# Idle products in four float32 passes of up to 384 columns, in place of one float32r pass of up to 512

## The chip, the cores and the metric

The kernel runs on one core of a Trainium2 chip. The core has five engines that work side by side and meet by semaphores: TensorE (PE in the profile; its weight loads are shown apart as PEld) multiplies matrices, VectorE (DVE), ScalarE (ACT) and GpSimd (POOL) work element by element, and SyncE (SP) issues most of the transfers. The metric is the time of one execution on the device in microseconds (us), less being better. Runs of the kernel before took 491.94 to 493.27 us, with a median of 492.61.

## What is computed

An attention layer of the RWKV-6 kind, then a channel mixer with a residual. The shapes are 4 batches, 8 heads, 768 time steps and a head of 48; the mixer works on 768 x 384 values a batch and widens them to 1536.

```
for t in range(S):                                  # state: (B, H, D, D), starts at 0
    cur = einsum('bhd,bhe->bhde', u * k[t], v[t])
    y[t] = einsum('bhd,bhde->bhe', r[t], state + cur)
    state = w[t][..., None] * state + einsum('bhd,bhe->bhde', k[t], v[t])
x  = y as (B, S, H * D)
xn = (x - mean(x)) / sqrt(var(x) + 1e-6) * g_ln
out = x + maximum(xn @ w_ch1, 0) @ w_ch2
```

## The kernel before

The work is cut into eight rounds: a batch and one half of its 768 steps, so 384 steps (three tiles of 128) for all eight heads. In each round the attention is computed in blocks of 64 steps. Within a block, pairs of sub-blocks are joined level by level (the tile `a` in PSUM takes the small products `a<-r,k`), the keys times the values give the state after each block (`a<-v,k`, then a scan `s` on VectorE), and `a<-v,A`, `a<-vx,A` and `a<-s,r` give the outputs. Then come the normalization (`xn`, its transpose `xT_ps`, and `xf`), the first product of the mixer into `h_ps`, the relu into `h`, and the second product into `o` with the residual. The first round loads and converts the weights of the mixer beside this (`raw`, `held`, `w1`, `ffn2`). In rounds 0 to 3 the second product is done with plain float32 operands (`o<-ffn,h`, 12 chunks for each of the three tiles of a round). In later stages products are split into parts of type float32r (`h_ps<-xhl,wh` and the like).

Every operation is entered into a plan with a cost, and the list `ORDER` (from line 76) fixes the order in which the operations are issued, on which engine each of them goes, and so what every engine's stream of instructions looks like. `Plan.order` (from line 241) goes through the list once, computes when each operation would start by the costs, and gives each tile its place. It also keeps a count of the instructions that TensorE has had (`count`), takes from it where the stream of instructions crosses an edge between pieces of `PIECE` = 256 instructions, and adds a wait where the piece would not have come (`fetches`). These computed times are used for three things that change the program: the places of tiles, the order of semaphore waits, and the idle products.

Idle products are products of zeros by zeros into a PSUM bank that nobody reads. Where the plan sees TensorE without work for more than 0.35 us, it puts n units of them (each 0.24 us by the plan; half as many for the time up to 5.9 us) ahead of the next operation of TensorE, and adds `4 * -(-n // 3)` to its count of instructions. The function `idle` near the end of the kernel makes the products. Before the change, it takes one width for all products of a run: 512 columns where n is divisible by 3, 384 where the remainder is 1, 256 where it is 2, and as many products of that width as fit. Their operand is `nought_r`, one zero a partition of type float32r, read with a stride of nothing as 128 x 128 weights and as the moving columns. `nought_r` is made by ScalarE from `nought`, which VectorE sets to zero as its first instruction. ScalarE's next instructions are a square root that brings its table in (`root`), the clearing of a PSUM tile, and a load of the first tile of k (`nat_k`) on its own queue.

All engine calls go through one helper, so nearly all instructions have line 47 in the profile, and groups are told apart by the names of their tiles.

## Time and profile before

| | us |
|---|---|
| median of 3 runs | 492.61 |
| lowest and highest | 491.94, 493.27 |
| the profiled execution | 492.7 |
| its span, first to last instruction | 490.9 |
| share of the TensorE clock granted | 0.999 |

The profile is of one execution. Its span leaves out 1.8 us around the first and the last instruction. A group's row gives the engine, the operation, the tiles as output<-inputs, the shape and the count, then the busy time in us and the mean length of one in ns, then the idle time of the engine just before, with what ended it. In the timeline the first number is the start and the second the length of the merged stretch, and square brackets hold the idle time before it and what ended it. "issue" means that an engine stood still and the profile shows nothing that it waited for. A window's row has, for each engine, the busy time and the number of instructions that ran in it, then the granted clock, the busy share of the DMA engines and GB/s. Products of TensorE overlap, and their ends are modelled. Queue 8 in the list of the DMA queues has the kind "instruction": it brings code. Semaphore waits that are instructions of their own stand in an engine's stream, but not in the counts of the views.

### The profile page before, as it was taken

To read this page: it belongs to the slowest core of one execution; us is meant where nothing else is said; L and a number is where in the kernel's file an instruction comes from. 1 tells how busy PE (TensorE), PEld (TensorE's weight loads), DVE (VectorE), ACT (ScalarE), POOL (GpSimd) and SP (SyncE) were. 2 spreads that over 40 slices of the span, in tenths; PEclk is the share of its full clock that TensorE was granted. 3 is DMA by queue.
4 is the path that set the end of the run, shared out by engine and by line. 5 is a ranking of instruction groups with operands and counts; after the bars stand their busy time and mean duration, and the time that the engine had idled before them with its cause. 6 is when DMAs were issued, how large, how long until landed. Compare 5 with 4: busy or idle time off the path is not lost.

```text
span 490.9 us, 17279 instructions
## 1 busy us (share of the span) xinstructions
PE 475.5 (97%) x7409; PEld 410.1 (84%) x7409; DVE 352.4 (72%) x727; ACT 257.5 (52%) x593; POOL 126.0 (26%) x136
## 2 busy tenths in 40 slices
PE   7898999999999999998999999999999999999995
PEld 6677988666987779976789877789999999999995
DVE  6999999999956838776776976856967552532544
ACT  5988888536452444372238515158753543533440
POOL 3113107033215163322115120001241241130210
PEclk9999999999999999999999999999999999999999
DMA  7887774675494831382572251053212210232201
GB/s 220 208 229 174 223 173 127 174 203 138 107 246 84 217 58 52 107 207 45 132 206 83 42 81 51 16 158 100 82 34 64 81 49 21 78 97 80 81 1 49
DMA packets 105469, 56.23 MB, mean 115 GB/s; under 512 B 61872, under 2 KB 102320, under 8 KB 105392
## 3 DMA queue, kind: packets, MB, share of 16 engines
q1 hardware_dynamic: 105120, 54.92, 43.0%
q8 instruction: 58, 0.95, 0.8%
q10 hardware_dynamic: 272, 0.20, 0.2%
q14 instruction: 19, 0.16, 0.1%
HBM read 45.27 MB, written 7.47 MB: 107 GB/s over the span
## 4 chain that ended last, share of the span: by engine, by line
PE 81%; DVE 11%; issue 2%; ACT 2%; DMA 1%; SPq 1%; POOL 1%; DVEq 0%; POOLq 0%
PE h_ps L47 27%; PE a L47 23%; PE o L47 19%; PE o_2P L47 3%; PE k_ps L47 2%; DVE A L47 2%; PE o_2D L47 2%; PE r_ps L47 2%; PE xT_ps L47 2%; DVE vals L47 2%; DMA raw<-in_moe_w_ch_dram 1%; DVE s L47 1%; PE kn_ps L47 1%; SPq L47 1%; DVE nat_k L47 1%
## 5 line engine op out<-in xcount | busy, mean ns | idle before, releaser
L47 PE MATMUL o<-ffn,h 128*128 128x384 f32 x288 | 100.4, 490 | 0.0
L47 ACT ACTIVATE h<-h_ps 128x384 f32<-128x384 f32 (+2 forms) x108 | 47.9, 456 | 67.5 <-PE h_ps L47 67.0
L47 PEld LDWEIGHTS o<-ffn,h 128*128 128x128 f32 x288 | 52.0, 190 | 28.3
L47 ACT ACTIVATE h_ps<-h_ps 128x384 f32<-128x384 f32 x84 | 39.2, 478 | 52.3 <-PE h_ps L47 51.0
L47 PE MATMUL h_ps<-xd,d 128*128 128x384 f32 x204 | 50.5, 354 | 0.7 <-DVE x L47 0.7
L47 POOL TENSOR_TENSOR hL<-h,hH 128x384 fp32r<-128x384 f32 x24 | 25.7, 1078 | 89.2 <-ACT hH L47 32.9
L47 DVE SCALAR_TENSOR_TENSOR hD<-hH,hL 128x384 fp32r<-128x384 f32 x48 | 31.0, 664 | 24.1 <-PE a L47 10.3
L47 PEld LDWEIGHTS a<-r,k 48*56 48x56 f32 (+3 forms) x3072 | 39.5, 122 | 9.7 <-issue 3.2
L47 PE MATMUL a<-r,k 48*56 48x32 f32 (+3 forms) x3072 | 43.6, 208 | 0.9 <-ACT k L47 0.9
L47 PE MATMUL h_ps<-xhl,wl 128*128 128x384 f32 x180 | 43.9, 352 | 0.0
L47 PE MATMUL h_ps<-xhl,wh 128*128 128x384 f32 x180 | 41.5, 338 | 0.1
L47 DVE TENSOR_TENSOR k<-k,tot 112x768 f32<-112x768 f32 (+1 forms) x40 | 31.5, 790 | 12.3 <-PE a L47 12.1
L47 DVE TENSOR_TENSOR r<-r,tot 112x768 f32<-112x768 f32 (+1 forms) x40 | 34.4, 863 | 6.6 <-PE a L47 5.1
L47 PEld LDWEIGHTS h_ps<-xd,d 128*128 128x128 f32 x204 | 35.5, 188 | 3.1 <-DVE x L47 1.0
L47 DVE TENSOR_TENSOR hL<-h,hH 128x384 fp32r<-128x384 f32 x24 | 13.8, 584 | 27.6 <-ACT hH L47 14.6
L47 PEld LDWEIGHTS h_ps<-xhl,wh 128*128 128x128 f32 x180 | 32.2, 188 | 0.5 <-issue 0.5
L47 PEld LDWEIGHTS h_ps<-xhl,wl 128*128 128x128 f32 x180 | 31.1, 188 | 1.4
L47 ACT COPY A<-a 32x384 f32<-32x384 f32 (+5 forms) x60 | 25.3, 426 | 7.2 <-PE a L47 5.4
L47 ACT ACTIVATE xf<-xT_ps,g_sb 128x384 f32<-128x384 f32 (+2 forms) x27 | 14.5, 547 | 27.1 <-PE xT_ps L47 20.4
L47 ACT ACTIVATE hH<-h 128x384 fp32r<-128x384 f32 x48 | 23.4, 518 | 6.9 <-issue 4.9
L47 PE MATMUL h_ps<-xf,w 128*128 128x128 f32 (+1 forms) x144 | 25.7, 332 | 0.0
L47 POOL TENSOR_TENSOR nat_r<-pad_k,pad_r 128x576 f32<-128x576 f32 (+1 forms) x9 | 15.0, 1668 | 40.5 <-DVE nat_k L47 38.3
(184 smaller groups left out, 1090.3 us busy)
## 6 DMA issues: line engine op xcount, KB each, us to landing
d<-w1d SPq DMA_DIRECT2D x84, 192.0 KB, 2.5
raw<-in_moe_w_ch_dram SPq DMA_DIRECT2D x24, 384.0 KB, 3.7
nat_w<-in_w_dram SPq DMA_DIRECT2D x24, 192.0 KB, 3.7
nat_r<-in_r_dram SPq DMA_DIRECT2D x24, 192.0 KB, 3.4
v<-in_v_dram SPq DMA_DIRECT2D x24, 192.0 KB, 3.9
nat_k<-in_k_dram SPq DMA_DIRECT2D x23, 192.0 KB, 3.4
w1d<-w1diff SPq DMA_DIRECT2D x12, 192.0 KB, 3.6
out_dram<-x SPq DMA_DIRECT2D x4, 576.0 KB, 4.8
```

The source lines that it names most:

```text
L47: ins = self.tc.keep_in_program_order(f(*args, **kw))
```

## The change

The zeros stay float32, the copy to float32r is dropped, and a run of n idle units is made of products of up to three units, 128 columns a unit.

```diff
     nought = const.tile([P, 1], F32, name="nought")
     DVE.memset(nought, 0.0)
-    nought_r = const.tile([P, 1], F32R, name="nought_r")
-    ACT.copy(out=nought_r, in_=nought)
+    zeros = nought.broadcast_to([P, P])
...
     def idle(n, home):
         t = banks.tile([P, 512], F32, tag=f"b{home}", name="idle")
-        cols = 512 - 128 * (n % 3)
-        for _ in range(max(n * 576 // (cols + 38), 1)):
+        while n:
+            now = min(n, TT)
             PE.matmul(
-                t[:, 0:cols], nought_r.broadcast_to([P, P]), nought_r.broadcast_to([P, cols]),
-                start=True, stop=True,
+                t[:, 0 : now * P], zeros, nought.broadcast_to([P, now * P]), start=True, stop=True
             )
+            n -= now
```

`TT` is 3 and `P` is 128. Nothing in the plan changes: neither `ORDER`, nor the costs, nor the number of units n of each run, nor the places of the tiles. Every other operation stays as it was and in its order.

## The prediction

> **What bounds the kernel now.** The page first, then the chain of waits, then the waits and the timeline at three places.

> ```profile
> span 490.9 us, 17279 instructions
> PE 475.5 (97%) x7409; PEld 410.1 (84%) x7409; DVE 352.4 (72%) x727; ACT 257.5 (52%) x593; POOL 126.0 (26%) x136
> q8 instruction: 58, 0.95, 0.8%
> PE 81%; DVE 11%; issue 2%; ACT 2%; DMA 1%; SPq 1%; POOL 1%; DVEq 0%; POOLq 0%
> ```

> TensorE (PE) carries 81% of the chain that ended last, VectorE (DVE) 11%. The idle products fill the first 40 us only, where the chain runs over VectorE and the loads:

> ```profile
> DVE rk L47 <- DMA nat_k<-in_k_dram: 2.6, 1, 2.6
> DVE pad_k L47 <- DMA nat_k<-in_k_dram: 0.6, 1, 0.6
> ```

> These are the two longest of VectorE's waits for data in the first 50 us; the third is for a load too, and none is for TensorE. So the idle products themselves lie on no path. The chain has 2% of "issue", about 10 us (0.02 x 490.9), and three pieces of it in the later part stand out:

> ```profile
> 194.42 0.13 issue
> ...
> 223.07 1.48 issue
> ...
> 327.81 0.72 issue
> ```

> The second, seen in the timeline:

> ```profile
> 222.42 0.64 PE L47 MATMUL a<-v,k 64*48 64x48 f32 x40
> 224.54 0.30 PE L47 MATMUL a<-v,k 64*48 64x48 f32 x8 [1.48 <-issue]
> 224.98 0.32 DVE L47 COPY s<-a 112x48 f32<-112x48 f32 x2 [3.83 <-PE a L47]
> ```

> One group of 48 products, all of whose inputs were there for the first 40, stops in its middle. That is no wait for data. The windows between the three points at which TensorE goes on tell what it is:

> ```profile
> core 0: us, PE busy (x) PEld busy (x) DVE busy (x) ACT busy (x) POOL busy (x), PEclk, DMA share, GB/s
> 194.50:224.50 30.00, 28.52 (x636) 24.37 (x636) 20.08 (x35) 16.80 (x37) 10.84 (x11) 1.00 0.58 147
> 224.50:328.50 104.00, 103.13 (x2165) 80.97 (x2165) 80.01 (x167) 42.40 (x94) 20.66 (x23) 1.00 0.35 85
> ```

> Products and weight loads are 2 x 636 = 1272 from the first point to the second and 2 x 2165 = 4330 from the second to the third. Queue 8 moved 0.95 MB in 58 packets, 16.4 KB each; TensorE's 2 x 7409 = 14,818 instructions over 58 are about 256 a packet. 5 x 256 is 1280 and 17 x 256 is 4352: both counts fall short by 8 and 22, and TensorE's stream also holds waits on semaphores, which the views do not count. So all three stops lie on one grid of 256 instructions: TensorE ran out of code at a piece's edge and waited for queue 8. From the edge before to the point where it goes on:

> ```profile
> 191.28:194.55 3.27, 3.14 (x148) 2.78 (x137) 1.68 (x6) 0.85 (x2) 1.07 (x2) 1.00 0.02 5
> 221.19:224.54 3.35, 1.88 (x136) 1.75 (x136) 0.00 (x0) 2.13 (x6) 0.81 (x2) 1.00 0.65 151
> 325.62:328.53 2.91, 2.19 (x131) 2.06 (x130) 0.63 (x2) 2.11 (x6) 1.09 (x3) 1.00 0.31 80
> ```

> A piece of code takes 2.9 to 3.35 us to come. Where 256 instructions take longer, the fetch is hidden; where small products run through them faster, TensorE stops. [...]

> **The change part by part.** First, the instructions. The diff turns each run of n idle units into products of three, so ceil(n/3) of them. I get n from the number and width of the products in each run: width 512 is n divisible by 3, 384 remainder 1, 256 remainder 2.

> ```profile
> L47 PE MATMUL idle<-nought_r x93: 273/380/792, 2.3 to 38.8; 128*128 128x512 f32 x52, 128*128 128x256 f32 x24, 128*128 128x384 f32 x17
> ...
> L47 PE MATMUL o<-ffn,h 128*128 128x384 f32 x288 | 100.4, 490 | 0.0
> ```

> The 15 runs have 28, 9, 5, 3, 3, 6, 1, 3, 1, 3, 9, 3, 15, 1 and 3 products; n is 27, 9, 4, 3, 2, 6, 1, 2, 1, 2, 7, 3, 8, 1 and 3. After: 9+3+2+1+1+2+1+1+1+1+3+1+3+1+1 = 31 products. A plain float32 product is two loads and two products in the trace: the second product of the network runs 4 rounds x 3 tiles x 12 chunks = 144 times and has 288 records. So 31 x 4 = 124 instructions stand where 93 x 2 = 186 stood. **62 instructions fewer** ahead of 40 us, and each later edge falls 62 instructions further into the program.

> What lies there? I count 62 instructions on from each edge and read the time to the next edge, on the times of before:

> ```profile
> 23.80:27.42 3.62, 3.61 (x128) 2.61 (x130) 3.62 (x12) 3.56 (x9) 0.00 (x0) 1.00 0.82 240
> 191.62:196.00 4.38, 4.25 (x146) 3.64 (x140) 2.93 (x12) 1.22 (x4) 2.19 (x3) 1.00 0.03 7
> 221.62:230.63 9.01, 7.53 (x143) 5.18 (x136) 5.62 (x16) 2.72 (x7) 0.38 (x1) 1.00 0.20 54
> 257.62:261.53 3.91, 3.91 (x128) 3.61 (x131) 2.33 (x3) 3.83 (x10) 1.38 (x1) 1.00 0.71 204
> 281.52:285.38 3.86, 3.86 (x147) 2.73 (x138) 3.02 (x13) 0.00 (x0) 2.52 (x3) 1.00 0.31 20
> 326.08:332.23 6.15, 5.43 (x145) 5.04 (x137) 1.02 (x2) 3.21 (x8) 1.09 (x3) 1.00 0.69 160
> 341.50:345.15 3.65, 3.65 (x142) 3.35 (x137) 3.65 (x10) 3.30 (x9) 1.15 (x3) 1.00 0.50 157
> ```

> The three bad places have, with the stops taken out, 4.1, 7.3 and 5.2 us: all over 3.35. The next shortest after 100 us are 3.86 and 3.91. The last row is an edge pair of before that ran without a stop in 3.65 us. So all three stops should go and none come.

> What they cost now: "issue" counts from the modelled end of the last product, while in a stream the next one starts long before that.

> ```profile
> L47 PE MATMUL a<-v,k 64*48 64x48 f32 x768 | 12.3, 208 | 2.3 <-issue 1.5 <-DVE s L47 0.5
> L47 PE MATMUL a<-s,r 48*64 48x48 f32 x640 | 13.6, 220 | 0.8 <-issue 0.7
> L47 PE MATMUL h_ps<-xhl,wh 128*128 128x384 f32 x180 | 41.5, 338 | 0.1
> ...
> 421.37 4.21 PE h_ps L47 x24
> ```

> So the loss is the idle time, plus a product's length, less a stream's step: 1.48 + 0.21 - 0.02 = 1.67 us; 0.72 + 0.22 - 0.02 = 0.92; 0.13 + 0.34 - 0.175 (4.21/24) = 0.29. **Together 2.9 us**; by the idle times alone 2.3. It should come through to the end, as what waits next is late because of TensorE: VectorE stood 3.83 us for the products above.

> Second, the front. One unit of 384 float32 columns costs two records of

> ```profile
> 88.27 3.87 PE o L47 x12
> ```

> 3.87/12 = 0.32 us, two passes over 384 columns, so 0.42 us for 1000 column passes. A run of n = 3 keeps its length (4 x 384 = 3 x 512 column passes). One of n = 2 has 4 x 256 in place of 3 x 256 and grows by 0.11 us, one of n = 1 has 512 in place of 384 and grows by 0.05; with the same for n = 4, 7 and 8 this is 0.7 us over nine runs, much of it ahead of waits that are there anyway:

> ```profile
> 28.78 1.49 ACT L47 COPY A<-a 16x256 f32<-16x256 f32 x4 [0.37 <-PE a L47]
> ...
> 33.06 0.40 PE L47 MATMUL a<-v,k 64*48 64x48 f32 x16 [0.55 <-DVE s L47]
> ```

> ScalarE can pass its 0.37 us on. The pair of edges at 23.80 to 27.42 has only 3.62 us while the loads crowd the DMA engines (share 0.82), so a stop of 0 to 1 us may arise there; queued behind it are the products that ScalarE copies at 28.78, and the wait at 33.06 takes 0.55 of it. Third, the removed copy:

> ```profile
> 0.72 1.28 ACT L47 ACT_TABLE_LOAD   x1 [0.72 <-PEq L1789]
> 0.80 0.06 DVE L47 MEMSET nought<- 128x1 f32 x1 [0.80 <-PEq L1789]
> 2.02 0.19 ACT L47 CAST nought_r<-nought 128x1 fp32r<-128x1 f32 x1
> 2.23 1.28 ACT L47 ACT_TABLE_LOAD   x1
> 5.99 0.35 ACT L47 COPY pad_k<-nat_k 128x192 f32<-128x192 f32 x1 [1.35 <-DMA nat_k<-in_k_dram]
> ```

> ScalarE loses 0.19 us and perhaps a table load of 1.28, since no third one follows in 593 operations; either way it then waits for nat_k, so this is nothing. A bound for a gain: its load of nat_k, queued behind, goes out up to 1.3 us sooner and spares the loads some 0.7 us, by half of that. The idle products start near 0.9 instead of 2.26 us, run their cold part (792 ns is the longest) earlier, and end no later than before. I take **+0.3 us for the front**, between -0.7 and +1.4.

> Sum: 492.7 of the profiled run - 2.9 + 0.3 = 490.1; the median of the runs is 0.1 lower, so **490.0**. Bounds: 492.6 - 2.9 - 0.7 = 489.0 and 492.6 - 2.3 + 1.4 = 491.7.

> **The rivals.** *The stops go, but nothing is gained*, because another wait takes their place or the fetch is late at other edges: for it, 3.86 us is only 0.5 above the slowest fetch seen; against it, 3.65 ran clean, and VectorE and ScalarE wait on TensorE behind the stops. It gives 492.6 + 0.3 = 492.9, no change. [...] *The front eats half*: longer runs and a stop at 27.4 us reach VectorE's chain in full, +1.4, and the gain is 2.3 - 1.4 = 0.9, so 491.7; for it the small slack of ScalarE at 28.78, against it VectorE's waits, none on TensorE.

> *The grid lands badly* is the slower one. The edges move by 186 less the new count. If a float32 product of zeros were one load and one product, 62 would stand, and the move would be 124. The same reading of the grid, with 3.3 us a piece, then has edge pairs only 1.4 to 2.2 us apart at five places, such as

> ```profile
> 139.19:141.30 2.11, 2.11 (x96) 1.93 (x96) 0.00 (x0) 1.35 (x3) 0.09 (x1) 1.00 0.88 239
> ```

> where 192 instructions of small products take 2.1 us, and costs 7.8 us: 492.6 - 2.9 + 7.8 = 497.5. From a move of about 88 on it loses more than before; between 32 and 70 the sum of stops is zero. Against it: 288 records for 144 products.

> **How the numbers follow.** The forecast has 0.76, no gain 0.09, half eaten 0.08, a bad grid 0.07. About 0.3%, 1.5 us, is what a measurement of this kernel can tell from no change, so faster means under 491.1. The forecast's own range is 489.0 to 491.7 and gives 0.73 to faster and 0.03 to same; half eaten gives 0.02 and 0.06, no gain 0.07 to same and 0.02 to slower, the bad grid 0.07 to slower: 0.75, 0.16 and 0.09. The range that holds 8 in 10 is 488.8 to 492.3.

> **What would show it.** Right: the idle group has 62 records, TensorE 7378 in all; the "issue" waits at a<-v,k (1.5) and a<-s,r (0.7) are gone and no other of over 0.5 us has come after 100 us; TensorE's lead over before is near zero at 100 us, 2 us at 230 and 2.9 at 330. Wrong: idle records of another count, new "issue" stops in groups of small products, or a lag of over 1 us at 60 us.

## The result and the profile after

| | before | after |
|---|---|---|
| median of 12 runs each, taken side by side | 492.88 us | 490.32 us |
| lowest and highest | 491.21, 496.14 | 488.86, 492.46 |
| the profiled execution | 492.7 | 491.96 |
| its span | 490.9 | 490.2 |

The ratio is 0.9949, with a 95% interval of 0.9924 to 0.9973: faster by 2.56 us, where 2.6 was predicted. The change was run a second time for the experiments: 490.45 us against 493.53, ratio 0.9937 (0.9903 to 0.9970). But the profiled execution of the change is 1.64 us above its median, and that matters below: one profile of each kernel would have shown a gain of 0.7 us only. First the page of the profile after: the span, the engines, the granted clock in 40 slices, queue 8 and the chain.

```profile
span 490.2 us, 17215 instructions
PE 477.5 (97%) x7378; PEld 407.1 (83%) x7378; DVE 353.8 (72%) x727; ACT 256.9 (52%) x591; POOL 125.4 (26%) x136
PEclk9899999999999999999999999999999999999999
q8 instruction: 58, 0.95, 0.8%
PE 82%; DVE 6%; DMA 6%; ACT 2%; SPq 1%; issue 1%; POOL 1%; DVEq 0%; POOLq 0%; ACTq 0%
```

TensorE has 7378 products, 31 fewer than before, and as many loads: 62 instructions fewer. "issue" went from 2% of the chain to 1%. The clock has one slice of 8, the second, from 12.3 to 24.5 us. The groups of the two kinds of product that had stopped, and of the idle products:

```profile
L47 PE MATMUL a<-s,r 48*64 48x48 f32 x640 | 13.4, 220 | 0.0
L47 PE MATMUL a<-v,k 64*48 64x48 f32 x768 | 12.1, 208 | 0.6 <-DVE s L47 0.3
...
L47 PE MATMUL idle<-nought x62: 272/486/1006, 0.9 to 40.1; 128*128 128x384 f32 x44, 128*128 128x128 f32 x10, 128*128 128x256 f32 x8
```

The 0.8 and 2.3 us of idle time that these two groups had before are 0.0 and 0.6, with no "issue" among the releasers. The timeline at the place where the group of 48 products had stopped for 1.48 us after 40 of them:

```profile
222.64 1.52 PE L47 MATMUL a<-r,k 48*60 48x32 f32 x96
223.98 0.73 PE L47 MATMUL a<-v,k 64*48 64x48 f32 x48
224.65 0.51 PE L47 MATMUL kn_ps<-ident,k 112*128 112x112 f32 x3
```

All 48 now run as one stretch of 0.73 us. To see where the time went, I match the products of TensorE, without the idle ones, of two traces by their order (7316 in each) and subtract the starts: a positive lead means that the kernel is ahead of the profiled execution of before. The second line is the profile of the second measurement of the change.

| lead in us, at (us of before) | 60 | 100 | 190 | 200 | 230 | 330 | 480 |
|---|---|---|---|---|---|---|---|
| the change, first profile | -1.29 | -1.95 | -1.88 | -1.50 | 0.13 | 0.75 | 0.74 |
| the change, second profile | 0.80 | 0.40 | 0.42 | 0.80 | 2.53 | 3.37 | 3.33 |

From 190 us on the two agree: the steps at 194.55, 224.54 and 328.53 us are 0.30, 1.66 and 0.89 us, 2.85 in all, the three stops of the prediction to within 0.03 us each. The front does not agree: by 100 us the first profile has lost 1.95 us, the second has gained 0.40. A part of this is a stop that the kernel before does not have, in another group of small products. First the timeline of the first profile, then the row of the second:

```profile
65.79 0.89 PE L47 MATMUL a<-r,k 48*32 48x32 f32 x79
67.26 0.32 PE L47 MATMUL a<-r,k 48*32 48x32 f32 x14 [0.59 <-issue]
```

```profile
64.91 0.32 PE L47 MATMUL a<-r,k 48*32 48x32 f32 x14 [0.21 <-issue]
```

It costs 0.77 us of the lead in the first and 0.39 in the second. The windows of the first profile show more of what was lost:

```profile
core 0: us, PE busy (x) PEld busy (x) DVE busy (x) ACT busy (x) POOL busy (x), PEclk, DMA share, GB/s
12.66:14.54 1.88, 0.00 (x1) 0.00 (x0) 1.78 (x4) 1.68 (x5) 0.00 (x0) 1.00 1.08 247
14.77:18.18 3.41, 3.41 (x42) 2.74 (x35) 3.38 (x8) 3.41 (x6) 1.55 (x3) 0.50 0.65 189
18.18:60.00 41.82, 39.58 (x968) 31.37 (x967) 40.80 (x98) 36.30 (x96) 9.39 (x12) 1.00 0.78 203
```

TensorE did nothing for 1.88 us, and just behind that its clock was half for 3.41 us, once. The timeline of the same execution says how the gap came about, with rows of ScalarE, then of TensorE, then of ScalarE again:

```profile
0.72 1.28 ACT L47 ACT_TABLE_LOAD   x1 [0.72 <-PEq L1788]
0.93 0.70 ACTq L47 DMA_DIRECT2D nat_k<-in_k_dram  x1
2.02 0.20 ACT L47 ACTIVATE root<-eps 128x1 f32<-128x1 f32 x1
...
10.55 2.11 PE L47 MATMUL idle<-nought 128*128 128x384 f32 x6
14.54 0.88 PE L47 MATMUL a<-r,k 48*60 48x32 f32 x32 [1.88 <-ACT k L47]
...
10.89 0.51 ACT L47 COPY pad_k<-nat_k 128x384 f32<-128x384 f32 x1 [4.71 <-DMA nat_k<-in_k_dram]
12.86 0.56 ACT L47 ACTIVATE w<-raw 128x384 f32<-128x384 f32 x1 [0.56 <-DMA raw<-in_moe_w_ch_dram]
13.92 0.57 ACT L47 COPY k<-k_ps 112x512 f32<-112x512 f32 x1
```

And the same place in the timeline of before, TensorE and then ScalarE's copy of k:

```profile
11.53 2.21 PE L47 MATMUL idle<-nought_r 128*128 128x512 f32 x9
14.64 0.57 PE L47 MATMUL a<-r,k 48*60 48x32 f32 x26 [0.89 <-ACT k L47]
...
14.01 0.58 ACT L47 COPY k<-k_ps 112x512 f32<-112x512 f32 x1
```

With the copy to float32r gone, its table load is gone too: one is left, and ScalarE's load of `nat_k` goes out at 0.93 us. The first tile is done sooner (its `k_ps` begins at 10.07 us in place of 11.13), and the run of nine idle units starts at 10.55 in place of 11.53. It has a fixed length, so it also ends 1.1 us earlier (12.66 against 13.74), while the products behind it wait for ScalarE's copy `k`, which starts only 0.09 us sooner (13.92 against 14.01). Ahead of that copy ScalarE waits for the second tile of k, until 10.89, and for a load of weights (`raw`), until 12.86. The cover over that wait became a hole.

### The profile page after: what moved, and what is told of

It reads as the page before. It is cut to its first block, busy times and chain, and to the rows that moved or that the text cites. A ratio compares the mean times of both kernels' runs of the same rounds, so it can differ in the third digit from the quotient of the medians.

```text
span 490.2 us, 17215 instructions
## 1 busy us (share of the span) xinstructions
PE 477.5 (97%) x7378; PEld 407.1 (83%) x7378; DVE 353.8 (72%) x727; ACT 256.9 (52%) x591; POOL 125.4 (26%) x136
## 4 chain that ended last, share of the span: by engine, by line
PE 82%; DVE 6%; DMA 6%; ACT 2%; SPq 1%; issue 1%; POOL 1%; DVEq 0%; POOLq 0%; ACTq 0%
PE h_ps L47 27%; PE a L47 23%; PE o L47 19%; DMA raw<-in_moe_w_ch_dram 5%; PE o_2P L47 3%; PE r_ps L47 2%; PE k_ps L47 2%; PE o_2D L47 2%; PE xT_ps L47 2%; PE kn_ps L47 2%; SPq L47 1%; DVE vals L47 1%; DMA vx<-v 1%; DVE x L47 1%; DVE A L47 1%
## 5 line engine op out<-in xcount | busy, mean ns | idle before, releaser
L47 PE MATMUL o<-ffn,h 128*128 128x384 f32 x288 | 100.4, 490 | 0.0
L47 ACT ACTIVATE h<-h_ps 128x384 f32<-128x384 f32 (+2 forms) x108 | 47.8, 455 | 65.6 <-PE h_ps L47 65.0
L47 PEld LDWEIGHTS o<-ffn,h 128*128 128x128 f32 x288 | 52.1, 190 | 28.3
L47 ACT ACTIVATE h_ps<-h_ps 128x384 f32<-128x384 f32 x84 | 39.2, 478 | 52.3 <-PE h_ps L47 51.0
L47 PE MATMUL h_ps<-xd,d 128*128 128x384 f32 x204 | 50.6, 354 | 0.7 <-DVE x L47 0.7
L47 PEld LDWEIGHTS a<-r,k 48*56 48x56 f32 (+3 forms) x3072 | 39.9, 122 | 12.6 <-issue 4.6
L47 POOL TENSOR_TENSOR hL<-h,hH 128x384 fp32r<-128x384 f32 x24 | 25.7, 1076 | 89.3 <-ACT hH L47 33.0
L47 DVE SCALAR_TENSOR_TENSOR hD<-hH,hL 128x384 fp32r<-128x384 f32 x48 | 31.0, 663 | 24.1 <-PE a L47 10.3
L47 PE MATMUL a<-r,k 48*56 48x32 f32 (+3 forms) x3072 | 44.2, 209 | 2.5 <-ACT k L47 1.9
L47 PE MATMUL h_ps<-xhl,wl 128*128 128x384 f32 x180 | 43.9, 352 | 0.0
L47 PE MATMUL h_ps<-xhl,wh 128*128 128x384 f32 x180 | 41.3, 337 | 0.0
L47 DVE TENSOR_TENSOR k<-k,tot 112x768 f32<-112x768 f32 (+1 forms) x40 | 31.6, 793 | 13.0 <-PE a L47 12.9
L47 DVE TENSOR_TENSOR r<-r,tot 112x768 f32<-112x768 f32 (+1 forms) x40 | 33.9, 850 | 6.7 <-PE a L47 5.2
L47 PEld LDWEIGHTS h_ps<-xd,d 128*128 128x128 f32 x204 | 35.5, 188 | 3.1 <-DVE x L47 1.0
L47 DVE TENSOR_TENSOR hL<-h,hH 128x384 fp32r<-128x384 f32 x24 | 13.8, 583 | 27.6 <-ACT hH L47 14.6
L47 PEld LDWEIGHTS h_ps<-xhl,wh 128*128 128x128 f32 x180 | 32.3, 188 | 0.0
L47 PEld LDWEIGHTS h_ps<-xhl,wl 128*128 128x128 f32 x180 | 31.1, 188 | 1.3
L47 ACT COPY A<-a 32x384 f32<-32x384 f32 (+5 forms) x60 | 25.3, 426 | 6.5 <-PE a L47 4.4
L47 ACT ACTIVATE xf<-xT_ps,g_sb 128x384 f32<-128x384 f32 (+2 forms) x27 | 14.5, 547 | 26.7 <-PE xT_ps L47 19.8
L47 ACT ACTIVATE hH<-h 128x384 fp32r<-128x384 f32 x48 | 23.4, 518 | 6.9 <-issue 4.9
L47 PE MATMUL h_ps<-xf,w 128*128 128x128 f32 (+1 forms) x144 | 25.7, 332 | 0.0
L47 POOL TENSOR_TENSOR nat_r<-pad_k,pad_r 128x576 f32<-128x576 f32 (+1 forms) x9 | 14.4, 1599 | 41.7 <-DVE nat_k L47 24.6
```

Of the source, the lines that this page charges most:

```text
L47: ins = self.tc.keep_in_program_order(f(*args, **kw))
```

## The experiments

All were timed in five rounds beside the kernel before: the first four on one chip, the next four on a second, the last two on a third. Medians of before were 492.82, 493.53 and 494.53 us, so times are compared within a batch or by their ratios.

**1. The edges put back, by products of 4 columns.** In the first run of idle units, 6 products of three units and 19 tiny ones take the place of 9, which is 64 instructions more; the edges then lie 2 instructions earlier than in the kernel before.

```diff
+    no = []
+
     def idle(n, home):
...
-        while n:
-            now = min(n, TT)
+        units, small = {0: (18, 19)}.get(len(no), (n, 0))
+        no.append(n)
+        while units:
+            now = min(units, TT)
...
-            n -= now
+            units -= now
+        for _ in range(small):
+            PE.matmul(t[:, 0:4], zeros, nought.broadcast_to([P, 4]), start=True, stop=True)
```

> The changed kernel with the first run of idle products made of 6 of 384 columns and 19 of 4 columns, in place of 9 of 384: 64 instructions of TensorE more, so that the edges of the 256-instruction pieces lie 2 from where they lay before the change; all products stay float32. If the edges made the gain: the stops in a<-v,k (1.5 us of issue) and a<-s,r (0.7 us) are back and the time is 490.3 + 2.9 = 493.2 us. If the four passes or the dropped copy made it: no stops there, 490.3 us.

Measured: 495.24 us, ratio 1.0032 (1.0007 to 1.0058). The timeline at the old place:

```profile
223.87 0.64 PE L47 MATMUL a<-v,k 64*48 64x48 f32 x39
226.34 0.33 PE L47 MATMUL a<-v,k 64*48 64x48 f32 x9 [1.83 <-issue]
```

The windows behind it, with the columns of the windows above:

```profile
227.00:228.00 1.00, 1.00 (x6) 0.59 (x5) 1.00 (x7) 0.44 (x1) 0.00 (x0) 0.95 0.06 16
228.00:229.00 1.00, 1.00 (x3) 0.61 (x2) 1.00 (x7) 0.00 (x0) 0.00 (x0) 0.50 0.00 0
230.00:231.00 1.00, 1.00 (x5) 0.84 (x4) 1.00 (x2) 0.25 (x1) 0.00 (x0) 0.50 0.00 0
231.00:232.00 1.00, 1.00 (x4) 0.58 (x3) 1.00 (x2) 0.33 (x1) 0.00 (x0) 0.84 0.00 0
```

The stop is back, after 39 products in place of 40: same zeros, same type, no copy, other edges. It cost more than its length, since the clock was half from 227.9 to 231.3 us behind it, another 1.67 us of the lead. The median is a less clean proof than the stop: the tiny products have a price of their own, as number 2 shows, and here too the clock was half from 12.87 to 16.28 us, where TensorE did not stand still. This profile ends 6.0 us behind the second profile of the change, and 1.8 us of that are there before 190 us, a new stop of 0.58 us at 105.93 included. The stop in `a<-s,r` did not come back, though its edge did: the packet of code had started 0.3 us ahead of that edge.

**2. The edges put where the prediction counted five new stops, by the same tiny products** (192 instructions more than in the change: `{0: (18, 35), 1: (0, 19)}` in the same lines).

> The changed kernel with 192 instructions of TensorE more in the first two runs of idle products (products of 4 columns), which puts the edges 126 instructions after those of before. If a piece takes 3.3 us to come and the edges decide: five stops of 1.1 to 1.9 us in groups of small products near 141, 183, 260, 275 and 313 us, 7.8 us together, so 490.3 + 7.8 = 498 us. If code is fetched in time anyway: 490.3 us.

Measured: 508.07 us, ratio 1.0284 (1.0248 to 1.0321). Most of this is another thing, seen in the windows of the front:

```profile
8.00:12.40 4.40, 4.40 (x42) 4.40 (x41) 3.26 (x8) 0.93 (x2) 1.70 (x4) 1.00 0.96 286
12.40:32.80 20.40, 20.40 (x121) 19.71 (x121) 7.43 (x14) 6.75 (x14) 1.95 (x5) 0.50 0.57 154
```

A row of the timeline there:

```profile
19.18 8.11 PE L47 MATMUL idle<-nought 128*128 128x4 f32 x38
```

TensorE is busy all the time, and its clock is half for 20.40 us. One record of a tiny product takes 0.21 us (8.11/38) at this clock, so the run was also far too long. The lag was 14.2 us by 60 us, and 1.6 more by the end. The experiment cannot price the five stops; number 6 does the same without tiny products. Its trace does show where TensorE stops: at two of the five places, for 1.49 us at 157.74 and 1.18 us at 278.76, with a clock of half from 159.15 to 162.56 us behind the first.

**3. The edges moved, but one float32r pass and the copy kept.** Every product of a run has 512 columns, and the first run has 23: 150 instructions in place of 186, so the edges lie 36 later than before.

```diff
-    zeros = nought.broadcast_to([P, P])
+    nought_r = const.tile([P, 1], F32R, name="nought_r")
+    ACT.copy(out=nought_r, in_=nought)
...
-        while n:
-            now = min(n, TT)
+        for _ in range({0: 23}.get(len(no), n)):
             PE.matmul(
-                t[:, 0 : now * P], zeros, nought.broadcast_to([P, now * P]), start=True, stop=True
+                t, nought_r.broadcast_to([P, P]), nought_r.broadcast_to([P, 512]),
+                start=True, stop=True,
             )
-            n -= now
+        no.append(n)
```

> The kernel before (float32r, one pass, the copy to float32r on ScalarE stays) with n products of 512 columns in each run and 23 in the first: 75 products, 150 instructions in place of 186, so the edges lie 36 instructions further on than before. If the edges made the gain: no stops in a<-v,k and a<-s,r, and 492.9 - 2.9 = 490.0 us without any four-pass product. If the four passes or the copy made it: 492.9 us.

Measured: 490.99 us, ratio 0.9951 (0.9928 to 0.9973), as good as the change. In the lead, the steps at the three places are 0.30, 1.66 and 0.89 us again. Smaller stops are new, at 66, 227 and 345 us, and cost 0.81, 0.89 and 0.42 us of the lead. The second is right behind the old place, as the timeline has it:

```profile
223.00 0.73 PE L47 MATMUL a<-v,k 64*48 64x48 f32 x48
...
226.96 0.44 PE L47 MATMUL xT_ps<-ident,xn 128*128 128x128 f32 x2 [0.72 <-issue]
```

So neither four passes nor float32 zeros make the gain; the number of instructions does. The 12 runs fall into six from 489.79 to 490.26 us and six from 491.73 to 492.18, and 11 of them have a mean clock of 0.997 or more. So times also differ by some 2 us for a reason other than the clock, which stays open.

**4. The gap at 14 us filled**: 17 units in place of 9 in the second run (12 instructions more: `{1: (17, 0)}`, no tiny products). It was run in two batches; the change itself was run beside the second.

> The changed kernel with 17 units in place of 9 in the second run of idle products (3 products and 12 instructions more, edges within the stretch without stops), which fills the gap of 2 us before 14.5 us. If the gap lets the clock fall to half from 14.8 to 18.2 us in some executions, as in the profiled one of the change: clock 0.999 or 1.0 in all, and a median of 489 to 489.6 us with a spread under 2 us. If the clock is not what spreads the times: 490.3 us and the same spread of 3.6 us.

> The changed kernel once more, for the spread of its times beside the next two runs. Both theories: median 489.8 to 490.8, lowest near 488.9 and highest near 492.4, as in its first 12 runs. If a halved clock behind the gap at 14 us makes that spread, its profile shows either a clock of 0.50 for one stretch of some 3.4 us near 15 to 18 us and a span of 489.5 to 490.5, or a clock of 1.00 throughout and a span near 488.

> The change with 17 units of idle work in place of 9 in the second run, once more. If the clock halves only because the gap before 14.6 us is open, the filled gap keeps it at 1.00 and the time at 489.3 to 490.3, with a spread of under 2 us. Rival (the gap has nothing to do with the spread): the same median and spread as the changed kernel beside it, some 3.5 us.

Measured: 490.46 us, ratio 0.9938 (0.9909 to 0.9968), and 490.20 us, ratio 0.9932 (0.9909 to 0.9955); the change beside it 490.45. The timeline of the first of them:

```profile
10.58 3.84 PE L47 MATMUL idle<-nought 128*128 128x384 f32 x12
14.35 0.64 PE L47 MATMUL a<-r,k 48*60 48x32 f32 x32
```

No gap, and the clock is 1.00 at 14 us and after. Yet the median is no better than that of the change, and the spread, under 2 us in the first batch, is 3.8 us in the second (489.06 to 492.86): the expectation on the spread fell. The clocks listed with the runs tell more than the spread. Of the 20 runs with the gap filled none has a mean clock under 0.997; of the 21 runs of the change 8 have (side by side on one chip it is none of 12 and 2 of 9).

The second profile of the change, with a span of 487.6 us, is one without the loss. The end of the gap in its timeline, with ScalarE's copy of k:

```profile
13.48 0.64 PE L47 MATMUL a<-r,k 48*60 48x32 f32 x32 [0.75 <-ACT k L47]
...
12.86 0.57 ACT L47 COPY k<-k_ps 112x512 f32<-112x512 f32 x1
```

And the window behind it:

```profile
13.48:18.18 4.70, 4.14 (x54) 2.98 (x54) 4.67 (x10) 4.70 (x10) 1.55 (x3) 1.00 0.88 242
```

There the second tile came at 10.47 us, ScalarE did not wait for `raw`, its copy of k started 1.06 us sooner than in the first profile, the gap was 0.75 us, and the clock stayed whole. So of the 2.35 us between the two profiles at 100 us, 1.06 are there at the end of the gap (14.54 against 13.48), before the clock falls; while it is half another 0.45 come, and the rest later, 0.38 of it at the stop near 65 us.

**5. The copy kept, its result unread.**

```diff
+    nought_r = const.tile([P, 1], F32R, name="nought_r")
+    ACT.copy(out=nought_r, in_=nought)
     zeros = nought.broadcast_to([P, P])
```

> The change with ScalarE's copy of the zeros put back, its result read by nobody. If the dropped copy opens the gap: ScalarE's load of nat_k goes out near 2.0 us again instead of 0.93, k_ps begins near 11.1 us instead of 10.07, the gap of TensorE before 14.6 us is near 1 us instead of 1.9, the clock stays at 1.00 and the time is 489.5 to 490.4 with a spread of under 2 us. Rival (the copy is nothing, as predicted): the load goes out as in the change, or the gap shrinks and the clock and the spread stay as in the changed kernel.

Measured: 490.58 us, ratio 0.9941 (0.9917 to 0.9964), 489.96 to 491.81. The copy alone decides when the load goes out, by ScalarE's part of the timeline:

```profile
2.02 0.19 ACT L47 CAST nought_r<-nought 128x1 fp32r<-128x1 f32 x1
2.02 0.71 ACTq L47 DMA_DIRECT2D nat_k<-in_k_dram  x1
2.21 1.28 ACT L47 ACT_TABLE_LOAD   x1
```

The second table load is back with it. Two parts of the expectation did not come: `k_ps` begins at 10.43 us (some 11.1 expected; 10.07 and 10.14 in the two profiles of the change), and the gap is 1.45 us, between the 1.88 and 0.75 of the change. So how much of the gap is due to the dropped copy is not shown. Two of 11 runs have a mean clock under 0.997. The profiled execution is 1.10 us behind the change's second profile, 0.80 of it in the front; by the medians the difference is 0.13 us, which these runs cannot tell from nothing.

**6. One unit a product**: `now = 1`, 79 products of 128 columns, 316 instructions. The edges lie where they lay in number 2, with idle products of the usual length.

> The change with one unit a product: 79 products of 128 columns in place of 31 of up to 384, 316 instructions in place of 124, so each later edge of the code falls 130 instructions earlier than before the change (or, the same, 192 earlier than with it). If a piece is asked for at its edge and takes 3.3 us: five new stops of 1.2 to 1.9 us, 7.8 us in all, 497.5 or so. If TensorE's queue asks for code up to 2 us ahead of the edge and two fetches stand 3.4 us apart at least: stops at two of the five places only, near 142 (1.7 us) and 262 us (1.4 us), 493 to 494. If edges do not matter: 490.3.

Measured: 496.67 us, ratio 1.0049 (1.0020 to 1.0078), from 492.80 to 501.56. The profiled execution is the slowest of them. Its timeline at two of the five places:

```profile
145.49 0.51 PE L47 MATMUL a<-r,k 48*60 48x32 f32 x10 [1.76 <-issue]
...
268.87 1.42 PE L47 MATMUL a<-r,k 48*60 48x32 f32 x46 [2.11 <-issue]
```

Two of the windows behind the first:

```profile
146.00:147.00 1.00, 1.00 (x42) 1.00 (x34) 0.79 (x1) 0.00 (x0) 0.00 (x0) 0.50 1.02 283
151.00:152.00 1.00, 1.00 (x3) 0.54 (x2) 1.00 (x1) 0.00 (x0) 0.00 (x0) 0.50 1.18 126
```

Against the change's second profile, the two stops take 1.97 and 2.32 us, at the places where the second theory had them, and at the other three places at most 0.30 us is lost. But at each the clock falls to half, for 6.83 us (from 145.17 and from 268.05 us), and from 140 to 160 us the kernel falls back by 4.96 us in all. Two more of the 12.0 us by which this execution ends behind the other are lost by 100 us, where a gap of 2.19 us and a half clock stand at 15 us. The expectation of 493 to 494 lacked this. The run with a clock of 1.000 took 492.80 us, the one with 0.980 took 501.56.

**7. Two units a product**: `now = min(n, 2)`, 44 products, 176 instructions; the edges lie 10 later than before.

> The change with up to two units a product: 44 products of up to 256 columns in place of 31 of up to 384, 176 instructions in place of 124, so the edges of the code lie 10 instructions later than before the change in place of 62; passes, units and the dropped copy as in the change. If the place of the edges is the gain: the stop in mid-group of a<-v,k near 223 us is back (lead 1.3 to 1.8 us lost there), the one in a<-s,r near 327 us at least in part (0 to 0.9 us), and the median is 492.0 to 493.5. Rival (the gain comes from the form of the idle products or from the dropped copy): no stops there, 490.0 to 490.8.

Measured: 493.31 us, ratio 0.9976 (0.9951 to 1.0001). That is the first theory's number, and the timeline has its rows:

```profile
221.50 0.73 PE L47 MATMUL a<-v,k 64*48 64x48 f32 x45
223.71 0.29 PE L47 MATMUL a<-v,k 64*48 64x48 f32 x3 [1.48 <-issue]
```

The stop is back, now after 45 products, with 1.68 us against the change; the other two are not. The zeros, their type and the dropped copy are those of the change, and more than half of its gain is gone.

**8. The gap made longer**: 3 units in the second run (`{1: (3, 0)}`).

> The change with 3 units of idle work in place of 9 in the second run (8 instructions fewer), so that the gap of TensorE before the first products of a near 13.5 us is about 2.6 us instead of 0.75 to 1.9. If a gap of some 2 us halves the clock: the profile has a clock of 0.50 for one stretch of about 3.4 us between 13 and 19 us, TensorE lags the change's undisturbed profile by 1.2 to 2.5 us at 60 us, and the median is 491.3 to 492.5. Rival (the halved clock came by chance, or VectorE and the loads hide it): clock 1.00 or the lag gone by 60 us, 490.0 to 490.8.

Measured: 490.99 us, ratio 0.9943 (0.9919 to 0.9967), between the two theories. The gap came, as the timeline shows:

```profile
13.89 0.64 PE L47 MATMUL a<-r,k 48*60 48x32 f32 x32 [2.31 <-ACT k L47]
```

But in this execution the clock stayed whole behind it:

```profile
13.89:18.18 4.29, 3.57 (x51) 2.71 (x52) 4.26 (x10) 4.29 (x9) 1.53 (x3) 1.00 0.85 232
```

So "a gap of 2 us halves the clock" is too strong as a rule. Over the runs there is a tendency: 10 of 12 have a mean clock under 0.997. But the change itself was not run on this chip, and the clock does not set the time alone: the times fall into six from 489.33 to 490.52 and six from 491.47 to 493.04, and four of the faster six are under 0.997 too.

## Why the prediction was right, step by step

**The stops that go.** Right in place, cause and size: 0.29, 1.67 and 0.92 us foreseen, 0.30, 1.66 and 0.89 measured. That the grid of 256 instructions decides is shown from three sides: the gain comes without four passes (number 3), it goes with them when the edges return (1 and 7), and the large stop moves through its group with the edges, after 40 products before, 39 with the edges 2 earlier, and 45 with the edges 10 later. A product and its load are two instructions, so 2 instructions are one product and 10 are five: the stop moves by exactly the number by which the edges move. The gaps of 8 and 22 in the prediction's count close as well: in the trace, with the waits of TensorE's stream counted, it goes on after 6850, 8130 and 12,482 instructions, exactly 5 x 256 and 17 x 256 apart, and in numbers 1 and 3 again after 8130. The count of 62 was right, and with it the rival of a move by 124 fell. The "two passes" that the prediction reads into one record of a float32 product rest on its length: in a stream, such a record of 384 columns takes 0.32 us (3.87/12), one of a product of float32r parts 0.175 (4.21/24): 1.8 times as long.

**The stop that comes.** "So all three stops should go and none come" failed in its second half. One came, near 65 us, for 0.39 and 0.77 us in the two profiles, and new "issue" stops in groups of small products are one of the prediction's own signs of being wrong. The prediction looked at pairs of edges after 100 us and at the one at 23.80, and not at this place. Its threshold would not have found it either: in the second profile the edges lie at 60.40 and 64.91 us, 4.5 us apart and not under 3.35, but the packet starts only at 62.34, 1.94 us behind its edge. The words "between 32 and 70 the sum of stops is zero" failed in the same way, as number 3 moves the edges by 36 and has three new stops.

**The grid of edges as a rule.** "A piece of code takes 2.9 to 3.35 us to come", asked for at its edge, was too simple. Over twelve traces the starts of the packets of queue 8 are never closer than 3.36 us (3.38 before, 3.48 in the first profile of the change), and they lie from 3.7 us ahead of the edge to 4.6 us behind it (3.1 to 4.6 before), with the edges counted in steps of 256 instructions from the stops. Where they start ahead, a pair of edges only 1.6 to 2.1 us apart runs without a stop of over 0.3 us, as at three of the five places of number 6; at the other two, where they start behind, TensorE stops for 1.8 to 2.1 us. The rival's price of 7.8 us for a bad grid was counted on five stops; by the medians it measured about 6 (496.67 against 490.45). In the profiled execution two stops and the clock behind them took 10, and the front 2. What makes a packet start ahead of its edge was not tried.

**The front: +0.3 us, of which the copy "is nothing".** Here another step failed, though the median hides it. "ScalarE ... either way it then waits for nat_k, so this is nothing" overlooked that ScalarE's own queue issues that load, and the load goes out 1.09 us earlier without the copy (0.93 against 2.02 in number 5). The bound did name this, and only as a gain. The slow start that the prediction calls the "cold part" is in the trace, where the first four records of idle products take 2.92 us from 0.91 us on, and the six from 10.55 us on 2.11. "End no later than before" was true and was taken for harmless; in the first profile the idle run ends 1.1 us earlier and the copy of k comes only 0.09 us sooner, and that is the gap at 14 us. With the copy kept the gap was still 1.45 us, so what share the copy has in it is open. What follows differs from one execution to the next: +0.40 us by 100 us in one, -1.95 in the other, which is outside the bound of 1.4. "A lag of over 1 us at 60 us", named as a sign that the prediction is wrong, did occur in the first profile (1.29) and not in the second.

The stretch at half clock in the first profile, 14.77 to 18.18 us, is 3.41 us long, behind a gap of 1.88 us; in numbers 1, 2 and 6 the clock was half in or behind stops of 1.49 to 2.11 us. Behind gaps of 1.45 us (number 5) and 2.31 us (number 8) it stayed whole. So the length of the gap alone does not decide, and why the clock falls with one gap and not with another is not shown.

**The sum.** 2.9 less 0.3 was expected, 2.56 and 3.08 came in the two batches. That the first is so close to 2.6 is luck: the stops that go are worth 2.85 us, but the new stop, the front (from -1.95 to +0.40 us with that stop) and the clock behind the old stops were not in the sum or not at their size, and they happen to cancel. The spread of both kernels goes in part with the clock. Of the 79 runs of before in the three batches, 28 have a mean clock of 0.998 or more and a median of 492.50 us; of the change's 21 runs 11 have, with 490.33. That leaves 2.2 us by the whole clock. That the rest is the halved clock behind the old stops, as in number 1, is likely, as in number 2 a stop of 1.49 us had a half clock behind it, and was not shown for the kernel before: in its profile the clock is whole behind the stop of 1.48.

**The rivals.** "Nothing is gained" fell with the steps of the lead. In the profile of before, queue 8 brings 58 packets and "issue" stops TensorE's products for 0.1 us or more four times, for 0.15 us at 104.74 and for 0.13, 1.48 and 0.72 us at the three places; those three were worth 2.85 us. "The front eats half" is what the first profile shows, and more than half, by the gap, the clock and the stop near 65 us and not by the causes that it named.

No version tried beats the change by more than these runs can tell; filling the gap gave 490.46 and 490.20.

## What to carry to other kernels

Where "issue" stops an engine, as it stopped TensorE here, in the middle of a group whose inputs are there, count instructions between such stops. If they are multiples of 256 with the semaphore waits (here 1280 and 4352), and a little less by the views (1272 and 4330), look at whether an edit adds or drops instructions ahead of them: 62 fewer moved them here, and with them came a half per cent (ratio 0.9949) that had nothing to do with what the edit is for. Undo the count alone before crediting the edit. Fillers of fixed length cover a wait only while their start stays where it was (here one ended 1.1 us earlier, and a gap of 1.88 us stood behind it), so look again at the gaps behind them when something ahead gets faster.
